# The opening of a fused attention and two-layer MLP kernel: units of 128 queries, keys turned by identity products, a new order

## The chip, the cores and the metric

One core of one Trainium2 chip runs the whole program. The metric is the device time of an execution in microseconds (us); the time before is the median of three runs.

## The reference

Attention over 4 batches, 8 heads, 768 tokens of 64 elements, in chunks of 32 queries; each chunk sees 8 memory tokens, 16 tokens to its left, its own 32 and 8 to its right. Then two dense layers on the 3072 tokens of 512 elements, 2048 wide inside; the weights come as 64-bit floats.

```python
for c in range(nc):
    scores = scale * np.matmul(q_c, k_full.transpose(0, 1, 3, 2))
    scores = scores - np.max(scores, axis=-1, keepdims=True)
    a = np.exp(scores)
    a = a / (np.sum(a, axis=-1, keepdims=True) + 1e-09)
    out[:, :, c_start:c_end] = np.matmul(a, v_full)
...
h = x @ w_in
g = np.maximum(0.01 * h, h)
x = g @ w_out
...
h = x @ w_in2
P = a[0] + a[1] * h + a[2] * h2 + a[3] * h3
Q = 1.0 + np.abs(b[0]) * np.abs(h) + np.abs(b[1]) * h2
g = P / (Q + 1e-06)
out = g @ w_out2
```

## The kernel before

Both layers run in 6 tiles of 512 tokens by 16 blocks of the hidden width. A block is one hidden product of 12 matmuls (`emit_h`, line 753: upper by upper, upper by lower and lower by upper halves of the operands, which are split into two roundings) and one output product of 12 matmuls (`emit_y`, line 811; `emit_o`, line 849, in the second layer). The order of every engine is the order in which the code is written (`manual_schedule`); nothing is planned by costs.

**The opening** is the attention of the first 512 tokens, 8 blocks of 64 queries (`FIRST`), taken two at a time as a unit `u`. For a block, `att_q` and `att_k` (lines 368, 378) turn queries (for two blocks at once) and 88 or 104 rows of keys by transposes on PE, and ACT copies them out. `att_b1` (line 460) makes the scores of 8 heads by 2 chunks in 16 small matmuls, and DVE takes the maximum and subtracts it (lines 469, 472), 256 columns at a time. For a unit, `unit_e` takes the exponential on ACT, `unit_n` normalises on DVE (lines 418 to 421), `unit_t` (line 428) turns the probabilities in four transposes, and ACT copies them in four pieces of 64 rows (line 433) into a block-diagonal tile, whose zeros POOL has set; `unit_x` (line 444) multiplies with the values over 128 rows. The result, x, is split into an upper half by ACT (line 447) and a lower half by DVE (line 448). `heat` (line 867) issues dummy products of the identity.

**The weight chain.** `pair_load` brings raw 64-bit words. A pair `n` holds two pieces, `ONE_` and `TWO_`: pair 0 the hidden blocks 0 and 1, pair 1 hidden block 2 and output block 0, pair 2 hidden 3 and output 1, pair 3 hidden 4 and output 2. Per piece: `pair_scale` (ACT, line 170), `pair_join` (DVE, three instructions, lines 177 to 180), `pair_hi` (ACT, line 188) rounds, `pair_lo` (DVE, line 194) subtracts. From pair 3 on, a pair is done in one go. Between the pieces stands `leaky`: two activations on ACT (lines 763, 764) and one subtraction on DVE (line 766) of a hidden block.

The order on PE behind the opening is: hidden blocks 0, 1, 2, output block 0, hidden 3, output 1, the turning of the next queries and keys, hidden 4. All loads are issued on the SP queue in the order written: queries and keys of all 8 blocks, the first weight piece, the values, the other weights. `copy_mem_v` on POOL puts the memory tokens' values into the value tiles ahead of their loads.

## Time and profile before

| | |
|---|---|
| median of three runs | 1149.4 us (1149.04 to 1150.69) |
| profiled execution | 1148.0 us, span 1146.2 us |
| PE busy | 1131.7 us, 99% of the span |
| DVE, ACT, POOL busy | 769.7, 631.8, 232.1 us |
| loads and stores | 131.98 MB, mean 115 GB/s |

The span runs from the first instruction to the last; the profiled execution's own time is 1.8 us longer. Times in rows count from the span's start. Busy PE means that a matmul is in flight, not that the array is full.

### The profile page before, as it was taken

What the parts mean: (1) busy time and instruction counts of PE and PEld (TensorE: products, weight loads), DVE (VectorE), ACT (ScalarE), POOL (GpSimd) and SP (SyncE); (2) the same over time, 40 slices, a digit from 0 to 9 for tenths busy, and PEclk for the clock granted to TensorE, in tenths of its full rate; (3) what the DMA queues carried; (4) which work ended last, traced back from release to release, by engine and by line L of the source; (5) the groups of instructions that cost most, each with busy time, mean ns of one, the idle gap of its engine ahead of it and who ended that gap; (6) DMA issues with size and microseconds to landing.
All of it is one profiled execution on the core that took longest, in us unless ns stands there. A gap on an engine that the chain in (4) does not pass through costs nothing.

```text
span 1146.2 us, 19651 instructions
## 1 busy us (share of the span) xinstructions
PE 1131.7 (99%) x7616; PEld 928.3 (81%) x7616; DVE 769.7 (67%) x1318; ACT 631.8 (55%) x1149; POOL 232.1 (20%) x264
## 2 busy tenths in 40 slices
PE   7999999999999999999999999999999999999998
PEld 6777788888888888888888888888888888888886
DVE  5887846555565555542345886887887888788775
ACT  4677632232232223223346876776777777777765
POOL 3000302231221322210000222222222222222222
PEclk9999999999999999999999999999999999999999
DMA  9966687797778777742342101001100100100101
GB/s 187 260 178 196 187 226 206 213 251 206 202 215 241 208 196 230 207 142 98 97 133 83 65 1 47 28 1 39 36 1 29 46 1 15 59 1 1 37 1 37
DMA packets 148472, 131.98 MB, mean 115 GB/s; under 512 B 63296, under 2 KB 118944, under 8 KB 148380
## 3 DMA queue, kind: packets, MB, share of 16 engines
q1 hardware_dynamic: 143372, 123.25, 37.6%
q0 software_dynamic: 4864, 7.45, 2.8%
q8 instruction: 60, 0.98, 0.4%
q14 instruction: 32, 0.26, 0.1%
q10 hardware_dynamic: 144, 0.03, 0.0%
HBM read 92.92 MB, written 37.75 MB: 114 GB/s over the span
## 4 chain that ended last, share of the span: by engine, by line
PE 95%; DVE 3%; ACT 1%; issue 1%; POOL 0%; DVEq 0%; POOLq 0%
PE hps L753 45%; PE acc L849 23%; PE acc L811 22%; PE psx L667 2%; PE pss L625 1%; PE pss L460 1%; PE hot L867 1%; DVE wwall L178 1%; PE psx L444 0%; PE psx L514 0%; DVE wwall L180 0%; PE psk L378 0%; DVE wwall L177 0%; ACT w L188 0%; DVE w L194 0%
## 5 line engine op out<-in xcount | busy, mean ns | idle before, releaser
L811 PE MATMUL acc<-g,w 128*128 128x512 f32 x1152 | 278.7, 391 | 0.1
L849 PE MATMUL acc<-w,g 128*128 128x512 f32 x1152 | 275.4, 389 | 0.0
L849 PEld LDWEIGHTS acc<-w,g 128*128 128x128 f32 x1152 | 216.2, 188 | 44.8
L811 PEld LDWEIGHTS acc<-g,w 128*128 128x128 f32 x1152 | 214.7, 188 | 46.1 <-ACT w L188 0.5
L763 ACT ACTIVATE g<-hps 128x512 fp32r<-128x512 f32 x96 | 57.4, 598 | 307.1 <-PE hps L753 307.1
L789 POOL TENSOR_TENSOR g<-R,g 128x512 fp32r<-128x512 f32 x96 | 124.2, 1294 | 504.4 <-ACT g L788 466.1
L753 PE MATMUL hps<-xh,w 128*128 128x512 f32 x768 | 209.0, 395 | 3.8 <-ACT pm L484 1.5
L753 PE MATMUL hps<-yh,w 128*128 128x512 f32 x768 | 204.1, 389 | 0.0
L766 DVE TENSOR_TENSOR g<-s,g 128x512 fp32r<-128x512 f32 x96 | 66.2, 690 | 177.6 <-ACT s L764 174.4
L753 PEld LDWEIGHTS hps<-xh,w 128*128 128x128 f32 x768 | 141.2, 188 | 34.6 <-ACT w L188 2.0
L753 PEld LDWEIGHTS hps<-yh,w 128*128 128x128 f32 x768 | 144.3, 188 | 29.9
L590 POOL DMA_DIRECT2D vb<-in_v_dram x128 | 83.2, 651 | 260.5 <-PE psx L667 207.9
L776 ACT ACTIVATE A<-hps 128x512 f32<-128x512 f32 x96 | 57.2, 596 | 113.9 <-PE hps L753 113.9
L792 DVE SCALAR_TENSOR_TENSOR A<-A,small,pb 128x512 f32<-128x512 f32 x96 | 72.0, 750 | 56.2 <-ACT pb L777 56.2
L753 PE MATMUL hps<-xl,w 128*128 128x512 f32 x384 | 103.0, 390 | 0.0
L753 PE MATMUL hps<-yl,w 128*128 128x512 f32 x384 | 102.6, 389 | 0.0
L783 DVE SCALAR_TENSOR_TENSOR A<-A,pb 128x512 f32<-128x512 f32 x96 | 66.5, 692 | 30.2 <-ACT pb L796 30.2
L753 PEld LDWEIGHTS hps<-xl,w 128*128 128x128 f32 x384 | 72.1, 188 | 15.7
L753 PEld LDWEIGHTS hps<-yl,w 128*128 128x128 f32 x384 | 72.1, 188 | 14.9
L778 ACT ACTIVATE R<-hps,small 128x512 f32<-128x512 f32 x96 | 75.0, 781 | 0.0
L785 DVE SCALAR_TENSOR_TENSOR R<-R,small,A 128x512 f32<-128x512 f32 x96 | 72.2, 752 | 3.4
L794 DVE SCALAR_TENSOR_TENSOR R<-R,small,hps 128x512 f32<-128x512 f32 x96 | 71.8, 748 | 3.4
(112 smaller groups left out, 1140.1 us busy)
## 6 DMA issues: line engine op xcount, KB each, us to landing
wr<-in_moe_w_in_dram SPq DMA_DIRECT2D x32, 512.0 KB
wr<-in_moe_w_out_dram SPq DMA_DIRECT2D x32, 512.0 KB
park_dram<-pb SPq DMA_DIRECT2D x16, 512.0 KB
pb<-park_dram SPq DMA_DIRECT2D x64, 128.0 KB
w_dram<-wwall SPq DMA_DIRECT2D x32, 256.0 KB
wb<-w_dram SPq DMA_DIRECT2D x32, 256.0 KB
kb<-in_k_dram SPq DMA_DIRECT2D x59, 112.0 KB
vb<-in_v_dram POOLq DMA_DIRECT2D x118, 56.0 KB, 3.3
```

What stands on the lines that cost most here:

```text
L590: nc.gpsimd.dma_start(out=vw[r + at:r + at + n, c], in_=v[bi, hs, lo:lo + n, :].rearrange("h p d -> p h d"))
L753: nc.tensor.matmul(ps[:, :n], w_[:, ws], x_[:, kk, :], start=(kk == 0 and m == 0), stop=(kk == KC - 1 and m == 2))
L763: nc.scalar.activation(out=gh, in_=ps, func=AF.Prelu, alpha=0.01)
L766: return [lambda: nc.vector.tensor_tensor(out=gl, in0=s, in1=gh.bitcast(F32), op=ALU.subtract)]
L778: nc.scalar.activation(out=R, in_=ps, func=AF.Identity, scale=ncf[:, 3:4], bias=ncf[:, 2:3])
L783: nc.vector.scalar_tensor_tensor(out=A0, in0=A0, scalar=ONE, in1=U0, op0=ALU.add, op1=ALU.mult)
L785: nc.vector.scalar_tensor_tensor(out=R0, in0=R0, scalar=ncf[:, 0:1], in1=A0, op0=ALU.add, op1=ALU.mult)
L789: nc.gpsimd.tensor_tensor(out=gl, in0=R0, in1=gh.bitcast(F32), op=ALU.subtract)
L792: nc.vector.scalar_tensor_tensor(out=A, in0=A, scalar=babs[:, 1:2], in1=U, op0=ALU.mult, op1=ALU.add)
L794: nc.vector.scalar_tensor_tensor(out=R, in0=R, scalar=ncf[:, 1:2], in1=ps, op0=ALU.add, op1=ALU.mult)
L811: nc.tensor.matmul(acc[i][d][:, :n], w_[:, ws], g_, start=(f == 0 and m == 0), stop=(f == FC - 1 and m == 2))
L849: nc.tensor.matmul(acc[i][s], g_[:, ss], w_, start=(f == 0 and m == 0), stop=(f == FC - 1 and m == 2))
```

## The change

The opening is taken in 4 units of 128 queries throughout. `unit_load` brings the keys of a unit in two loads, as packets of two tokens (512 B instead of 256 B); even and odd tokens then lie side by side in a row, and `turned` transposes them by ordinary products with a square of the identity, 16 for rows of 44 (56 and 44 in unit 0) and 16 for rows of 32. ACT copies them out in three pieces, interleaved. In `unit_s` the two chunks of a head stand side by side in a bank of 512 columns, so that maximum, subtraction, sum and product of a unit are one instruction each. The turned probabilities are copied whole by one instruction (`unit_t`), and `unit_x` multiplies each chunk by itself over 64 rows, 32 products into two banks. The zero tiles and most dummy products go. The order of the opening is new; half of the values is loaded ahead of the first weight piece. In the weight chain the subtractions of `leaky` 0, 1 and 2 and of the second piece of pair 1 go from DVE to POOL, and other steps change places.

```diff
-    room = [t[:, n] for t in early for n in range(4)]
-    rooms = {"k": kb + room[0:6], "v": vb + room[6:12], "q": room[12:16]}
+    rooms = {"k": kb, "v": vb + [early[1][:, n] for n in (2, 3)] + [early[2][:, n] for n in range(4)]}
...
+    TT = 2
+    KA, KB = (QB + LCTX) // TT + NM, QB // TT
+    KU = (CTX // TT, CTX // TT + LCTX // 4)
...
+    kroom = [two(kall), two(early[0][:, 0:2]), two(early[0][:, 2:4]), two(early[1][:, 0:2])]
+    qroom = [early[3][:, u].rearrange("p h d -> p (h d)") for u in range(4)]
+    kTs = [kT, kT2, kT34[:, 0], kT34[:, 1]]
+    half = lambda t, n: t.rearrange("p a b c d e -> p (a b c d e)")[:, n * 512:(n + 1) * 512]
+    opm = [mall.rearrange("p b c m -> p (b c m)"), mall2.rearrange("p b c m -> p (b c m)"),
+           half(pall, 0), half(pall, 1)]
+    opt = [pmore.rearrange("p n a b c d e -> p (n a b c d e)")[:, u * 512:(u + 1) * 512] for u in range(4)]
+    oqT, ops = {}, {}
...
+    def unit_load(u):
+        at = 2 * QB * u
+        pairs = lambda x, lo, n: x[0, :, lo:lo + n, :].rearrange("h (p t) d -> p h (t d)", t=TT)
+        flat = lambda t: t.rearrange("p h t d -> p h (t d)")
+        nc.sync.dma_start(out=early[3][:, u], in_=q[0, :, at:at + P, :].rearrange("h p d -> p h d"))
+        lo = max(at - LCTX, 0)
+        row, n = (lo - at + LCTX) // TT, at - LCTX + 96 - lo
+        nc.sync.dma_start(out=flat(kroom[u][row:row + n // TT]), in_=pairs(k, lo, n))
+        nc.sync.dma_start(out=flat(kroom[u][P // 2:P // 2 + KB]), in_=pairs(k, at - LCTX + CTX, QB))
+        if u == 0:
+            nc.sync.dma_start(out=kroom[u][48:48 + NM, :, 0, :], in_=mem_k[0].rearrange("h p d -> p h d"))
...
+    def turned(ps, t, r0, rows):
+        for p in range(NP):
+            for i in range(TT):
+                r = slice(r0, r0 + rows[i])
+                for e in range(2):
+                    nc.tensor.matmul(ps[e * 64:e * 64 + 64, p, i, :rows[i]], t[r, 2 * p + e, i, :], ident[r, r],
+                                     start=True, stop=True)
...
+    def unit_ka(u):
+        rows = (48 + NM, CTX // TT) if u == 0 else (CTX // TT, CTX // TT)
+        ps = psw.tile([P, 512], F32, tag="ps", name="psk")[:, :NP * TT * rows[0]]
+        ps = ps.rearrange("p (c t m) -> p c t m", c=NP, t=TT)
+        turned(ps, kroom[u], 0, rows)
+        a, b = kTs[2 * (u % 2)], kTs[2 * (u % 2) + 1]
+        O = QB // TT
+        def first():
+            if u == 0:
+                for t in (a, b):
+                    nc.scalar.copy(out=ends(t), in_=ps[:, :, 0, 48:].unsqueeze(2).to_broadcast([P, NP, 2, NM]))
+            nc.scalar.copy(out=a[:, :, NM:NM + CTX].rearrange("p c (m t) -> p c m t", t=TT),
+                           in_=ps[:, :, :, :CTX // TT].rearrange("p c t m -> p c m t"))
+            nc.scalar.copy(out=b[:, :, NM:NM + CTX - QB].rearrange("p c (m t) -> p c m t", t=TT),
+                           in_=ps[:, :, :, O:CTX // TT].rearrange("p c t m -> p c m t"))
+        return first
+    def unit_kb(u):
+        ps = psw.tile([P, 512], F32, tag="ps", name="psk")[:, :NP * QB]
+        ps = ps.rearrange("p (c t m) -> p c t m", c=NP, t=TT)
+        turned(ps, kroom[u], P // 2, (KB, KB))
+        b = kTs[2 * (u % 2) + 1]
+        return lambda: nc.scalar.copy(out=b[:, :, NM + CTX - QB:NM + CTX].rearrange("p c (m t) -> p c m t", t=TT),
+                                      in_=ps.rearrange("p c t m -> p c m t"))
...
+    def unit_s(u, b):
+        if b == 0:
+            ops[u] = psa.tile([P, 512], F32, tag="acc", name="pss").rearrange("p (b i c m) -> p b i c m", b=2, i=2, c=2)
+        ps, qt, kt = ops[u], oqT[u], kTs[2 * (u % 2) + b]
+        for p in range(NP):
+            for e in range(2):
+                r = slice(e * 64, e * 64 + 64)
+                for c in range(2):
+                    o = e * 64 + (p % 2) * CHUNK
+                    at = b * QB + c * CHUNK
+                    nc.tensor.matmul(ps[o:o + CHUNK, b, p // 2, c, :], qt[r, p, at:at + CHUNK],
+                                     kt[r, p, c * KOFF:c * KOFF + WIN], start=True, stop=True)
+    def unit_m(u):
+        ps = ops.pop(u)
+        if u == 0:
+            nc.vector.memset(ps[:, 0, :, 0, NM:NM + LCTX], NEG)
+        ps = ps.rearrange("p b i c m -> p (b i c) m")
+        mx = tmp.tile([P, 2 * NP, 1], F32, tag="mx", name="mx")
+        nc.vector.tensor_reduce(out=mx, in_=ps, op=ALU.max, axis=AX.X, negate=True)
+        nc.vector.tensor_tensor(out=opm[u].rearrange("p (n m) -> p n m", m=WIN), in0=ps,
+                                in1=mx.to_broadcast([P, 2 * NP, WIN]), op=ALU.add)
...
+    def unit_t(u):
+        ps = psa.tile([P, 512], F32, tag="acc", name="pst")
+        for i in range(4):
+            nc.tensor.transpose(ps[:, i * P:(i + 1) * P], opm[u][:, i * P:(i + 1) * P], ident)
+        return lambda: nc.scalar.copy(out=opt[u], in_=ps)
...
+    def unit_x(u, pool, tag):
+        ps = [pool.tile([P, 512], F32, tag=tag, name="psx")[:, :NP * QB].rearrange("p (n b m) -> p n b m", n=NP, b=2)
+              for c in range(2)]
+        pt = opt[u].rearrange("p (b i e h m) -> p b i e h m", b=2, i=2, e=2, h=2)
+        for b in range(2):
+            vt = rooms["v"][2 * u + b]
+            for p in range(NP):
+                for c in range(2):
+                    r = slice(c * SB, c * SB + SB)
+                    for e in range(2):
+                        nc.tensor.matmul(ps[c][e * 64:e * 64 + 64, p, b, :], vt[r, 2 * p + e, :],
+                                         pt[r, b, p // 2, e, p % 2, :], start=True, stop=True)
+        xh, xl = (x[:, :, 2 * QB * u:2 * QB * (u + 1)].rearrange("p n (b c m) -> p c n b m", b=2, c=2) for x in xt[0])
+        def upper():
             for c in range(2):
+                nc.scalar.copy(out=xh[:, c], in_=ps[c])
+        def under():
+            for c in range(2):
+                nc.vector.tensor_tensor(out=xl[:, c], in0=ps[c], in1=xh[:, c].bitcast(F32), op=ALU.subtract)
+        return upper, under
...
+    def leaky(c, eng=nc.vector):
...
-        nc.vector.memset(kb[0][0:32], 0.0)
+        nc.vector.memset(kroom[0][0:32], 0.0)
...
+        U = FIRST // 2
+        for u in range(U):
+            unit_load(u)
+        for j in range(4):
+            load_v(j)
         pair_load(0, ONE_)
+        xt[0] = (xpool.tile([P, KC, NMAX], F32R, tag="xh", name="xh"),
+                 xpool.tile([P, KC, NMAX], F32R, tag="xl", name="xl"))
+        heat(6)
+        unit_q(0)
+        key_a = unit_ka(0)
+        key_b = unit_kb(0)
+        key_a()
+        key_b()
+        for t in (2, 3):
+            nc.gpsimd.tensor_copy(out=ends(kTs[t]), in_=ends(kT))
+        copy_mem_v(early[2][:, 0:3])
+        for j in range(4, FIRST):
             load_v(j)
         pair_load(0, TWO_)
         pair_load(1)
         heat(2)
+        unit_s(0, 0)
+        unit_q(1)
+        unit_s(0, 1)
+        key_a = unit_ka(1)
+        key_a()
+        unit_m(0)
+        unit_e(0)
+        key_b = unit_kb(1)
+        unit_q(2)
+        key_b()
+        unit_n(0)
+        unit_s(1, 0)
+        key_a = unit_ka(2)
+        key_a()
+        unit_s(1, 1)
+        key_b = unit_kb(2)
+        key_b()
+        unit_m(1)
+        unit_e(1)
+        unit_s(2, 0)
+        unit_s(2, 1)
+        unit_m(2)
+        key_a = unit_ka(3)
+        key_a()
+        unit_q(3)
+        turned_p = unit_t(0)
+        key_b = unit_kb(3)
+        key_b()
+        turned_p()
+        unit_e(2)
+        unit_n(1)
+        unit_s(3, 0)
+        unit_s(3, 1)
+        turned_p = unit_t(1)
+        turned_p()
+        unit_m(3)
+        x0 = unit_x(0, psw, "ps")
+        x0[0]()
+        unit_n(2)
+        unit_e(3)
+        x1 = unit_x(1, psw, "ps")
+        turned_p = unit_t(2)
+        turned_p()
         pair_scale(0, ONE_)
+        unit_n(3)
+        x1[0]()
+        x0[1]()
+        turned_p = unit_t(3)
+        turned_p()
+        run(pair_join(0, ONE_))
+        x2 = unit_x(2, psa, "acc")
+        x2[0]()
+        pair_hi(0, ONE_)
+        pair_lo(0, ONE_)
+        x3 = unit_x(3, psa, "acc")
+        x3[0]()
+        x3[1]()
+        x1[1]()
+        x2[1]()
...
+        nc.gpsimd.memset(pall, 0.0)
...
         emit_h(0)
         pair_scale(0, TWO_)
-        pair_scale(1, ONE_)
         run(pair_join(0, TWO_))
         pair_hi(0, TWO_)
+        pair_scale(1, ONE_)
+        pair_lo(0, TWO_)
         run(pair_join(1, ONE_))
-        pair_lo(0, TWO_)
-        steps = leaky(0)
+        run(leaky(0, nc.gpsimd))
         pair_hi(1, ONE_)
         pair_scale(1, TWO_)
         pair_lo(1, ONE_)
         emit_h(1)
         run(pair_join(1, TWO_))
-        run(steps)
-        steps = leaky(1)
         pair_hi(1, TWO_)
         pair_scale(2, ONE_)
-        pair_lo(1, TWO_)
+        pair_lo(1, TWO_, nc.gpsimd)
+        run(leaky(1, nc.gpsimd))
         emit_h(2)
         run(pair_join(2, ONE_))
-        run(steps)
-        steps = leaky(2)
+        run(leaky(2, nc.gpsimd))
         pair_hi(2, ONE_)
         pair_scale(2, TWO_)
         pair_lo(2, ONE_)
         run(pair_join(2, TWO_))
-        run(steps)
         pair_hi(2, TWO_)
         pair_scale(3)
         pair_lo(2, TWO_)
```

On PE, in the middle of the opening (`kT`, `kT_105`, `kT_106` are turned keys, `pm` and `pb` probabilities, `hot` dummies). Before:

```order
L368 MATMUL psq<-ident,early 128x128 x4
L378 MATMUL psk<-ident,early 128x88 x8
L867 MATMUL hot<-ident 128x128
L428 MATMUL pst<-ident,pm_105 128x128 x4
L460 MATMUL pss<-kT,qT 32x64 x16
L460 MATMUL pss<-kT_106,qT 32x64 x16
L867 MATMUL hot<-ident 128x128 x4
L428 MATMUL pst<-ident,pm 128x128 x4
L444 MATMUL psx<-pb,vb 64x64 x16
L867 MATMUL hot<-ident 128x128 x2
```

and now:

```order
L423 MATMUL psk<-ident,early 64x44 x16
L470 MATMUL pss<-kT_106,qT 32x64 x16
L423 MATMUL psk<-ident,early 64x32 x16
L470 MATMUL pss<-kT,qT 32x64 x16
L470 MATMUL pss<-kT_105,qT 32x64 x16
L423 MATMUL psk<-ident,early 64x44 x16
L429 MATMUL psq<-ident,early 128x128 x4
L498 MATMUL pst<-ident,pm 128x128 x4
L423 MATMUL psk<-ident,early 64x32 x16
L470 MATMUL pss<-kT_106,qT 32x64 x32
L498 MATMUL pst<-ident,pm_104 128x128 x4
```

The turning of probabilities (`pst`) stood ahead of the next unit's scores (`pss`); now the scores of units 1 and 2 stand ahead of the first of them, and the keys (`psk`) take two groups of 16 between them.

On DVE, in the weight chain from the second piece of pair 1 on (`wr_93` pair 1, `wr_94` pair 2, `w` the lower half, `g` the hidden block). Before:

```order
L194 TENSOR_TENSOR w<-wwall,w 128x512 x2
L177 TENSOR_SCALAR wwall<-wwall 128x512
L178 SCALAR_TENSOR_TENSOR wwall<-wr_93,wwall 128x512
L180 SCALAR_TENSOR_TENSOR wwall<-wr_93,wwall 128x512
L766 TENSOR_TENSOR g<-s,g 128x512
L194 TENSOR_TENSOR w<-wwall,w 128x512
L177 TENSOR_SCALAR wwall<-wwall 128x512
L178 SCALAR_TENSOR_TENSOR wwall<-wr_94,wwall 128x512
L180 SCALAR_TENSOR_TENSOR wwall<-wr_94,wwall 128x512
L766 TENSOR_TENSOR g<-s,g 128x512
L194 TENSOR_TENSOR w<-wwall,w 128x512
L177 TENSOR_SCALAR wwall<-wwall 128x512
```

and now, from the lower half of pair 0's second piece on:

```order
L194 TENSOR_TENSOR w<-wwall,w 128x512
L177 TENSOR_SCALAR wwall<-wwall 128x512
L178 SCALAR_TENSOR_TENSOR wwall<-wr_93,wwall 128x512
L180 SCALAR_TENSOR_TENSOR wwall<-wr_93,wwall 128x512
L194 TENSOR_TENSOR w<-wwall,w 128x512
L177 TENSOR_SCALAR wwall<-wwall 128x512
L178 SCALAR_TENSOR_TENSOR wwall<-wr_93,wwall 128x512
L180 SCALAR_TENSOR_TENSOR wwall<-wr_93,wwall 128x512
L177 TENSOR_SCALAR wwall<-wwall 128x512
L178 SCALAR_TENSOR_TENSOR wwall<-wr_94,wwall 128x512
L180 SCALAR_TENSOR_TENSOR wwall<-wr_94,wwall 128x512
L194 TENSOR_TENSOR w<-wwall,w 128x512
```

The subtractions into `g` have left DVE, and so has one into `w`; two joins now stand in a row.

On POOL, behind the copies of the memory values, now (before, two memsets stood there and then the loads of later values):

```order
L345 COPY early<-early 32x1024
L968 COPY kT_106<-kT 128x4x2x8 x2
L345 COPY early<-early 8x1536
L345 COPY early<-early 32x1536
L1043 MEMSET pb 128x1024
L833 TENSOR_TENSOR g<-s,g 128x512
L194 TENSOR_TENSOR w<-wwall,w 128x512
L833 TENSOR_TENSOR g<-s,g 128x512 x2
L656 DMA vb<-in_mem_v_dram 8x4x64
```

The four subtractions stand behind the memset of the probabilities' tile.

## Rows read from the trace of the kernel before

**Rows 1.** Page, parts 1 and 4: busy time of each engine; the chain by engine.

```profile
PE 1131.7 (99%) x7616; PEld 928.3 (81%) x7616; DVE 769.7 (67%) x1318; ACT 631.8 (55%) x1149; POOL 232.1 (20%) x264
...
PE 95%; DVE 3%; ACT 1%; issue 1%; POOL 0%; DVEq 0%; POOLq 0%
```

**Rows 2.** Waits of PE, 54 us to the end: us in total, times, longest.

```profile
PE hps L753 <- ACT pm L484: 1.5, 2, 0.8
```

**Rows 3.** Timeline of PE, 0 to 57 us: start, us, what, count, idle before.

```profile
5.28 0.93 PE L378 MATMUL psk<-ident,kb 104*128 104x104 f32 x4
...
13.34 0.60 PE L368 MATMUL psq<-ident,early 128*128 128x128 f32 x4
13.78 0.86 PE L378 MATMUL psk<-ident,early 88*128 88x88 f32 x8
...
16.07 0.63 PE L428 MATMUL pst<-ident,pm 128*128 128x128 f32 x4 [1.17 <-DVE pm L421]
16.63 1.10 PE L460 MATMUL pss<-kT,qT 64*32 64x64 f32 x64
...
34.49 1.19 PE L753 MATMUL hps<-xh,w 128*128 128x512 f32 x4 [0.47 <-ACT xh L447]
...
54.29 1.20 PE L753 MATMUL hps<-xh,w 128*128 128x512 f32 x4 [1.33 <-ACT w L188]
```

**Rows 4.** Timeline of DVE, 0 to 62 us.

```profile
1.55 0.48 DVE L873 MEMSET kb<- 32x512 f32 x1 [0.16 <-issue]
...
12.48 0.43 DVE L469 TENSOR_REDUCE mx<-pss 128x4 f32<-128x256 f32 x1 [1.88 <-PE pss L460]
...
14.08 0.68 DVE L418 TENSOR_REDUCE sm<-pm 128x8 f32<-128x512 f32 x1
...
15.23 0.69 DVE L421 TENSOR_TENSOR pm<-pm,sm 128x512 f32<-128x512 f32 x1
17.35 0.43 DVE L469 TENSOR_REDUCE mx<-pss 128x4 f32<-128x256 f32 x1 [1.42 <-PE pss L460]
...
23.45 0.42 DVE L472 TENSOR_TENSOR pm<-pss,mx 128x256 f32<-128x256 f32 x1
...
34.47 0.42 DVE L448 TENSOR_TENSOR xl<-psx,xh 128x256 fp32r<-128x256 f32 x1 [0.35 <-ACT xh L447]
35.04 0.43 DVE L177 TENSOR_SCALAR wwall<-wwall 128x512 uint32<-128x512 uint32 x1
...
36.84 0.42 DVE L177 TENSOR_SCALAR wwall<-wwall 128x512 uint32<-128x512 uint32 x1
...
49.95 0.69 DVE L177 TENSOR_SCALAR wwall<-wwall 128x1024 uint32<-128x1024 uint32 x1 [0.35 <-ACT wwall L170]
```

**Rows 5.** Timeline of ACT, 0 to 62 us.

```profile
26.50 1.50 ACT L433 COPY pmore<-pst 64x256 f32<-64x256 f32 x4 [1.90 <-PE pst L428]
...
41.92 0.62 ACT L188 CAST w<-wwall 128x512 fp32r<-128x512 f32 x1
42.45 0.67 ACT L170 ACTIVATE wwall<-wr 128x512 f32<-128x512 f32 x1
...
53.19 1.04 ACT L188 CAST w<-wwall 128x1024 fp32r<-128x1024 f32 x1 [2.31 <-DVE wwall L180]
```

**Rows 6.** Timeline of PE: probabilities times values, three forms of the product.

```profile
26.34 1.15 PE L444 MATMUL psx<-pb,vb 128*64 128x64 f32 x32
...
173.44 1.41 PE L667 MATMUL psx<-pm,vb 64*64 64x32 f32 x64
...
195.07 1.14 PE L667 MATMUL psx<-pm,vb 64*64 64x32 f32 x64
```

**Rows 7.** Line 789 on POOL: shortest, median, longest in ns, first and last start.

```profile
L789 POOL TENSOR_TENSOR g<-R,g x96: 1283/1294/1307, 623.7 to 1138.1; 128x512 fp32r<-128x512 f32 x96
```

**Rows 8.** Windows: length, PEclk (granted clock), DMA share, GB/s.

```profile
2.00:16.00 14.00, 1.00 1.10 195
16.00:38.00 22.00, 1.00 1.06 275
```

More of the change, by code (lines that the diff above doesn't have):

```diff
@@ L379, in att_k @@
         pv = ps[:, :NP * rows].rearrange("p (c m) -> p c m", c=NP)
-        nc.scalar.copy(out=keys(j)[:, :, NM:NM + CTX], in_=pv[:, :, :CTX])
+        nc.scalar.copy(out=kT[:, :, NM:NM + CTX], in_=pv[:, :, :CTX])
         if j % BPS == 0:
-            for t in (kT, kT2) if j == 0 else (kT,):
-                ends = t.rearrange("p c (g m) -> p c g m", m=NM)[:, :, 0:KW // NM:KW // NM - 1, :]
-                nc.scalar.copy(out=ends, in_=pv[:, :, KLOAD:].unsqueeze(2).to_broadcast([P, NP, 2, NM]))
+            nc.scalar.copy(out=ends(kT), in_=pv[:, :, KLOAD:].unsqueeze(2).to_broadcast([P, NP, 2, NM]))
     def att_a(j):
```

141 lines of the change are left out of this document (26 added, 115 removed).

## The prediction

> **What bounds the kernel now.** I read the page first: the busy times and the chain of waits [rows 1]. TensorE (PE) is busy 99% of the span and 95% of the chain lies on it, so work taken off another engine is worth something only where PE waits for it. The waits of PE after 54 us [rows 2] show how little that is later: their largest group is 1.5 us, the next is the wait of 1.33 that ends at 54.29 [rows 3]. So nearly all that can be won lies ahead of 54.29, where PE starts hidden block 4 of the first layer [rows 3]. I call that start **the gate**: behind it both programs have PE's instructions in the same order, so the time changes by what the gate moves.
>
> In the timelines of PE, VectorE (DVE) and ScalarE (ACT) up to the gate, the reader sees two stretches. The opening (attention of the first 512 queries) has a period of 4.86 us per pair of blocks (DVE's first maximum at 12.48, then 17.35 [rows 4]), of which DVE works 3.4; the rest is the detour over PE, where the turning of the probabilities (16.07) stands ahead of the next scores (16.63) and waits for DVE's last product [rows 3]. The last subtraction of a row's maximum ends at 23.45 + 0.42 = 23.87, the last lower half of x at 34.47 + 0.42 = 34.89 [rows 4]. Then the weight chain: DVE joins the words of six weight pieces, ACT rounds them, DVE subtracts; it ends in ACT's rounding of pair 3 at 53.19 [rows 5], which releases the gate 1.1 us later.
>
> **Step 1, scores: 2.6 us earlier.** The first keys come later. Their tile's memset has 1024 columns instead of 512, twice 0.48 [rows 4], and the keys' load waits for it, with every later load behind it on SP; one more load stands ahead of mem_k. That is 0.5 to 0.9 us behind the 5.28 of before [rows 3]; I take 5.9. Loads after that don't bind at first: before, the load engines moved 195 GB/s [rows 8]; a unit of 128 queries now brings 0.33 MB of keys in pieces of 512 B for 0.39 MB in pieces of 256 B.
>
> From 5.9 PE itself sets the pace, because the scores no longer stand behind the turning of probabilities. Turning keys by identity products takes 16 products of about 44x64 by 44 columns, and 16 by 32 columns, per unit, where eight transposes took 0.6 (13.78, 0.86 with its drain [rows 3]). No row has this form. Below: 32 products of 64x64 by 32 columns took 1.14 and 1.41 with a drain of 0.1 (195.07, 173.44 [rows 6]), so 16 take 0.52 at best. Above: 16 of 128x64 by 64 columns took 1.15, again with its drain (26.34 [rows 6]): 1.09 as I count it. I take 0.75 and 0.62, nearer to the first, whose size is closer. The scores keep their sizes, and two groups of 16 took 1.10 [rows 3]; but neighbours in the order now write the same 32 rows of the bank where they wrote different ones. Bounds 0.52 and again 1.09; I take 0.65, nearest to the unchanged shape.
>
> Sum on PE: unit 0's keys at the slow rate of the first 7 us (four transposes at 5.28 took 0.93, eight at 13.78 took 0.86 [rows 3]) 1.3, then 0.62; two dummy products 0.55; three query turnings of 0.44 (13.34 to 13.78 [rows 3]); three times 0.75 and three times 0.62 for keys; one turning of probabilities 0.55; eight score groups of 0.65: 13.65 us, to 19.55; with 0.15 of waiting for ACT's key copies 19.7. DVE keeps up: three units of maximum and subtraction at 1.45 and two normalisations at 1.76 from 10.5 end at 18.4. Unit 3's maximum and subtraction over 512 columns take 0.7 each, as the 512-wide sum (0.68 [rows 4]): 21.2 against 23.87. Eight pieces of 256 become four of 512, which by itself saves DVE only 0.3 per unit.
>
> **Step 2, from there to x: 1.5 us.** DVE then does two normalisations (14.08 to 15.92 [rows 4], 1.76 each from start to next start, 3.5), two lower halves of x over 256 columns (0.42 each, of which I let 0.09 lie under the next one), the join of the first weight piece (1.85), waits 0.8 for ACT's rounding, subtracts (0.6), and six lower halves (2.0): 9.5 to 30.7, against 11.0 before. What goes is the stall behind four copies of 64 rows each, 1.50 for one pair [rows 5]; one whole copy of 512 columns replaces them. Next late here is unit 3's product with the values: PE turns its probabilities at 24.9, works 2 x 1.25 for units 2 and 3 (between 1.04 and 1.31, the two rows of the same form [rows 6]), ACT copies until 28.7, the moment at which DVE gets there. The values of unit 3 are the last load: 1.05 MB of queries, 1.29 of keys, 0.52 of weights and 1.79 of values at 195 GB/s end at 25.9, under one us ahead of their product.
>
> **Step 3, the weight chain: 1.3 us longer.** Four subtractions go to GpSimd (POOL), four times 0.6 off DVE. But now DVE has nothing to put between a join and the subtraction that waits for ACT. Five joins of 1.84 (35.04 to 36.84 [rows 4], and a handover) 9.2; pair 3's join, twice as wide, 3.2 (49.95 [rows 4] to 53.19 [rows 5]); four subtractions 2.4; four waits for ACT's 0.62 rounding with its handovers [rows 5], 0.68 each, 2.7; one wait for rounding and scaling in a row (0.62 and 0.67 [rows 5]), 1.3; one for pair 3's scaling 0.5. Together 19.3, and 0.1 to 0.2 of starts; before, 35.04 to 53.19 was 18.15. Behind each of DVE's waits stand the next joins, and behind those PE's hidden blocks. PE isn't late in between: its product for output block 0 waits for POOL's first weight subtraction until about 41, the gate has 1.1 us of slack over that path.
>
> A subtraction on POOL takes 1.29 [rows 7]. What it costs DVE, no row of the opening shows: nothing as the lower bound, 1.29 each as the upper (DVE standing still meanwhile). I take 0.2 in all: the 96 later ones took 1283 to 1307 ns whatever ran beside them [rows 7].
>
> The dummy products that go, the memsets that go from POOL (its copies of memory values, ahead of the last values' loads on SP, end near 11 us, before SP is there) and the first-value loads ahead of the first weights lie beside other work: PE is fuller than before without the dummies, and the granted clock reads 1.00 from 2 to 38 us [rows 8], also past PE's gap of 1.17 us ahead of 16.07 [rows 3].
>
> **Sum.** 2.6 + 1.5 - 1.3 - 0.2 = 2.6 us. The profiled execution took 1148.0 with a span of 1146.2; the median of three is 1149.4. From the median: 1146.8. A difference under 0.2%, 2.3 us, can't be told from none here, so the forecast lies just past that edge.
>
> **Rivals.**
> (a) *Nothing that can be told.* Scores at 0.75 instead of 0.65 cost 0.8, keys in the middle of their bounds 0.9: about 1148.5; values 0.5 late at unit 3 add as much. For it: three prices that no row has, none with slack behind it. Against: the sizes are nearest to the cheap rows. 0.38.
> (b) *Slower, PE becomes the bound.* At the upper price, 1.09, eight score groups cost 8 x 0.44 and the seven warm groups of key products about 7 x 0.4 more, 6.3 in all: 1153.1. It decides from 41% of that price on, where the gain is gone. Against: scores and key products have half the rows and no more columns than the dear row. 0.07.
> On this the Trainium skill ("TensorE: Matmul & The Clock Gate", The mechanism) has a rule: a weight load overlaps with matmuls in flight only when the row group differs. All sixteen key products of a group lie in one row group. By that rule case (b) would be the likelier for the keys; the dear row, with all 128 rows, bears it out, no row of 64 does.
> (c) *Slower, POOL holds DVE up.* If DVE stands still for the four subtractions, 4 x 1.29 = 5.2 is lost, 0.2 of it counted above: 1151.8; from about half of that on the gain is gone. For it: the joins beside them read two operands from SBUF, and one of the four gates PE's output block 0. Against: the narrow spread in rows 7. 0.07.
> The Trainium skill ("GPSIMD Engine Reference", Specifications) states just that: GpSimd's SBUF interfaces are shared with VectorE, with contention against instructions that have two SBUF inputs. It gives no price, and no trace here has that pair side by side.
>
> **How the numbers follow.** The forecast has 0.48, (a) 0.38, (b) and (c) 0.14 together. The forecast's own range: scores and keys at their lower bounds give 2.0 more and POOL free 0.2, so 1144.6, to 1147.1, where the edge lies. The range goes from 1144.2, a little below, for an earlier first key, through all of (a) to 1150.4, half of (b) or (c). Faster 0.48, same 0.38, slower 0.14.
>
> **What would show it.** Right: the gate near 51.7; the last subtraction of a maximum ending near 21.2, the last lower half of x near 30.7, and 19 to 20 us from there to the rounding of pair 3, with DVE waiting for ACT four times 0.7. PE without a gap between the first keys and unit 3's scores. Wrong: score groups or key products near 1.1; a gap ahead of unit 3's value product (loads); DVE's joins longer than 1.84 while POOL works; or any new wait of PE behind the gate.

## The result and the profile after

The changed kernel took 1163.58 us (median of 4, 1160.22 to 1167.66) against 1149.4: ratio 1.0123, interval 1.0082 to 1.0163. It is slower by 14 us; 1146.8 was forecast. The profiled execution took 1160.95 with a span of 1158.6, 12.4 more than before, and the gate (PE L820 here) moved from 54.29 [rows 3] to 65.88, 11.6 later. So the loss lies ahead of the gate, where the prediction had put the gain.

The page of the changed kernel, its part 1 (to be held against [rows 1]), and the windows of PE in it (length, busy with count, granted clock, DMA share, GB/s; against [rows 8]):

```profile
PE 1144.0 (99%) x7920; PEld 937.2 (81%) x7920; DVE 770.2 (66%) x1308; ACT 628.4 (54%) x1144; POOL 235.6 (20%) x267
```

```profile
2.00:16.00 14.00, 12.68 (x259) 0.88 1.05 188
16.00:38.00 22.00, 20.84 (x512) 0.57 0.89 245
38.00:46.00 8.00, 7.27 (x77) 0.50 1.16 277
```

PE has 304 records more (7920 for 7616), all in the opening. The granted clock, 1.00 in these stretches before, is at its lower level (0.50, which is 1.2 GHz) from 10 to 12 us and from 20 to 46 us. The timeline of PE in the changed kernel answers to [rows 3]:

```profile
6.47 2.18 PE L423 MATMUL psk<-ident,kb 56*64 56x56 f32 x64 [1.32 <-DMA kb<-in_mem_k_dram]
...
15.18 0.69 PE L470 MATMUL pss<-kT,qT 64*32 64x64 f32 x32
15.79 1.13 PE L423 MATMUL psk<-ident,early 44*64 44x44 f32 x32
16.85 0.69 PE L470 MATMUL pss<-kT,qT 64*32 64x64 f32 x32
17.47 1.11 PE L423 MATMUL psk<-ident,early 32*64 32x32 f32 x31
19.25 0.21 PE L423 MATMUL psk<-ident,early 32*64 32x32 f32 x1 [0.67 <-issue]
19.39 1.95 PE L470 MATMUL pss<-kT,qT 64*32 64x64 f32 x64
21.27 1.94 PE L423 MATMUL psk<-ident,early 44*64 44x44 f32 x32
...
26.89 1.95 PE L470 MATMUL pss<-kT,qT 64*32 64x64 f32 x64
...
65.88 1.21 PE L820 MATMUL hps<-xh,w 128*128 128x512 f32 x4 [1.36 <-ACT w L188]
```

Sixteen key products (32 records: each product makes two) take 1.06 us at the full clock (15.79 to 16.85) and 1.87 at the lower (21.27 to 23.14). Unit 3's scores end at 28.77. DVE in the changed kernel, its last maximum, its last lower halves of x and the joins beside POOL (against [rows 4]):

```profile
1.66 0.91 DVE L944 MEMSET kb<- 32x1024 f32 x1 [0.26 <-issue]
...
29.66 0.69 DVE L480 TENSOR_TENSOR pb<-pss,mx 128x512 f32<-128x512 f32 x1
...
40.08 2.08 DVE L521 TENSOR_TENSOR xl<-psx,xh 128x256 fp32r<-128x256 f32 x6 [0.23 <-ACT xh L517]
42.08 0.42 DVE L177 TENSOR_SCALAR wwall<-wwall 128x512 uint32<-128x512 uint32 x1
42.53 0.69 DVE L178 SCALAR_TENSOR_TENSOR wwall<-wr,wwall 128x512 uint32<-128x512 uint32 x1
43.26 0.69 DVE L180 SCALAR_TENSOR_TENSOR wwall<-wr,wwall 128x512 uint32<-128x512 uint32 x1
...
52.10 1.03 DVE L177 TENSOR_SCALAR wwall<-wwall 128x512 uint32<-128x512 uint32 x1 [1.26 <-ACT wwall L170]
53.17 1.79 DVE L178 SCALAR_TENSOR_TENSOR wwall<-wr,wwall 128x512 uint32<-128x512 uint32 x1
55.00 1.65 DVE L180 SCALAR_TENSOR_TENSOR wwall<-wr,wwall 128x512 uint32<-128x512 uint32 x1
```

and POOL and ACT beside them (the second against [rows 5]):

```profile
51.57 1.28 POOL L194 TENSOR_TENSOR w<-wwall,w 128x512 fp32r<-128x512 f32 x1 [3.07 <-ACT w L188]
53.12 2.98 POOL L833 TENSOR_TENSOR g<-s,g 128x512 fp32r<-128x512 f32 x2 [0.27 <-ACT s L831]
```

```profile
64.78 1.04 ACT L188 CAST w<-wwall 128x1024 fp32r<-128x1024 f32 x1 [2.31 <-DVE wwall L180]
```

The three instructions of a join sum to 1.80 us at 42.08 and to 4.47 at 52.10, while POOL subtracts. From the first join behind x to pair 3's rounding it is 22.7 us (42.08 to 64.78) where it was 18.15.

### The profile page after: what moved, and what is told of

It is laid out like the page before. It is cut to its first block, busy times and chain, and to the rows that moved or that the text cites. A ratio compares the mean times of both kernels' runs of the same rounds, so it can differ in the third digit from the quotient of the medians.

```text
span 1158.6 us, 20243 instructions
## 1 busy us (share of the span) xinstructions
PE 1144.0 (99%) x7920; PEld 937.2 (81%) x7920; DVE 770.2 (66%) x1308; ACT 628.4 (54%) x1144; POOL 235.6 (20%) x267
## 4 chain that ended last, share of the span: by engine, by line
PE 95%; DVE 2%; ACT 1%; DMA 1%; issue 1%; SPq 0%; DVEq 0%
PE hps L820 45%; PE acc L916 23%; PE acc L878 22%; PE psx L734 2%; PE pss L692 1%; PE psk L423 1%; PE pss L470 1%; DVE wwall L178 0%; PE psx L511 0%; PE pss L534 0%; PE psx L581 0%; DVE wwall L180 0%; DMA pb<-park_dram 0%; DVE wwall L177 0%; DMA park_dram<-pb 0%
## 5 line engine op out<-in xcount | busy, mean ns | idle before, releaser
L820 PE MATMUL hps<-xh,w 128*128 128x512 f32 x768 | 211.4, 399 | 5.8 <-ACT w L188 3.2
L820 PE MATMUL hps<-yh,w 128*128 128x512 f32 x768 | 204.1, 389 | 0.0
L820 PEld LDWEIGHTS hps<-xh,w 128*128 128x128 f32 x768 | 142.7, 190 | 37.7 <-ACT w L188 3.8
L820 PEld LDWEIGHTS hps<-yh,w 128*128 128x128 f32 x768 | 144.2, 188 | 30.0
L820 PE MATMUL hps<-xl,w 128*128 128x512 f32 x384 | 104.1, 393 | 0.0
L820 PE MATMUL hps<-yl,w 128*128 128x512 f32 x384 | 102.6, 389 | 0.0
L820 PEld LDWEIGHTS hps<-xl,w 128*128 128x128 f32 x384 | 72.5, 189 | 16.3 <-DVE xl L521 0.5
L820 PEld LDWEIGHTS hps<-yl,w 128*128 128x128 f32 x384 | 72.1, 188 | 14.9
```

The costliest lines, as they stand in the source:

```text
L820: nc.tensor.matmul(ps[:, :n], w_[:, ws], x_[:, kk, :], start=(kk == 0 and m == 0), stop=(kk == KC - 1 and m == 2))
```

## The experiments

Medians, and ratios to the kernel before on the same chip. The runs were made in five batches (e1 to e4, e5 to e8, e9 to e12, e13 to e15, e16 and e17), each on a chip of its own; the median of the kernel before was 1148.70 to 1149.14 in all of them, so a difference of medians between batches is good to about half a us, beside the runs' own spread. Traces show one execution of each.

| run | us | ratio, interval |
|---|---|---|
| e1 weight chain of before | 1157.04 | 1.0077 (1.0049 to 1.0104) |
| e2 dummies in the change | 1166.06 | 1.0149 (1.0119 to 1.0179) |
| e3 keys of before | 1150.54 | 1.0014 (1.0005 to 1.0024) |
| e4 before without dummies | 1148.42 | 0.9999 (0.9989 to 1.0008) |
| e5 keys and chain of before | 1146.58 | 0.9980 (0.9971 to 0.9990) |
| e6 e3, subtractions on DVE | 1149.59 | 1.0003 (0.9993 to 1.0012) |
| e7 key products by turns | 1192.91 | 1.0381 (1.0365 to 1.0397) |
| e8 e7, chain of before | 1189.3 | 1.0347 (1.0332 to 1.0362) |
| e9 equal rows, by turns | 1155.98 | 1.0065 (1.0049 to 1.0080) |
| e10 equal rows, in turn | 1157.8 | 1.0083 (1.0065 to 1.0102) |
| e11 e5, POOL subtracts | 1150.03 | 1.0011 (1.0000 to 1.0021) |
| e12 e5, three dummies | 1148.0 | 0.9994 (0.9984 to 1.0004) |
| e13 e5, many small dummies | 1156.84 | 1.0067 (1.0043 to 1.0092) |
| e14 e5, few large dummies | 1152.86 | 1.0028 (1.0015 to 1.0041) |
| e15 e5 again | 1146.74 | 0.9977 (0.9968 to 0.9987) |
| e16 e5, four wide dummies | 1147.87 | 0.9996 (0.9985 to 1.0007) |
| e17 e13, places apart | 1155.47 | 1.0053 (1.0033 to 1.0073) |

**Halves undone: e1, e3, e5.** e1 is the change with the weight chain's order and its subtractions as before:

```diff
-        run(leaky(0, nc.gpsimd))
+        steps = leaky(0)
...
-        pair_lo(1, TWO_, nc.gpsimd)
+        pair_lo(1, TWO_)
```

> The changed kernel with the weight chain written as before (the four subtractions back on DVE, steps in the old places). Theory POOL: the subtractions on POOL slow DVE's joins beside them (1.03, 1.79, 1.65 us where 0.42, 0.69, 0.69 stood) and leave waits; with them back the joins return to 0.42, 0.69, 0.69, the chain from the last lower half of x to the rounding of pair 3 goes from 22.7 to 18 to 18.5 us, and the time is 4 us less than the change, about 1159. Theory clock alone: the chain lengthens only as far as PE is late, the time stays within 1 us of the change's for like clocks.

e3 loads and turns the keys as before, one token a packet, and leaves the rest of the change:

```diff
-        turned(ps, kroom[u], 0, rows)
...
+            nc.tensor.transpose(ps[:, p * rows:(p + 1) * rows], s[:rows, p * P:(p + 1) * P], ident[:rows, :rows])
```

> The changed kernel with keys loaded in packets of one token and turned by transposes as before; the rest is the change's. Theory PE price: groups of keys take 0.3 us of PE instead of 1.06 at full clock, scores of unit 3 come 5 to 6 us earlier, time 1153 to 1157. Theory clock: with even less work on PE and no dummies the clock still falls to 0.50 somewhere between 10 and 45 us, and half of the gain or more is lost: 1156 to 1162.

e5 has both edits.

> The change with both suspects undone: keys turned four at a time by transposes as before, and the weight chain in the order of before with its subtractions on DVE. Theory (two separate costs that add up): e3 had its last xl end at 33.6 us, 1.3 us ahead of the kernel before, and lost 22.5 - 18.9 = 3.6 us in the chain behind it; with the chain of before the gate comes 3.6 us ahead of e3, near 53.9, and the time near 1147 us (1146 to 1148.5), 2 us below the kernel before. Rival (the costs are not separate: the narrow score and value products hold TensorE at the lower granted clock and this alone sets the gate): time stays within 1 us of e3, 1149.5 to 1151.5.

Against the change, the chain of before gives 6.5 us, the keys of before 13.0, both 17.0. In e1 the joins read 0.42, 0.69 and 0.69 again and the chain takes 18.9 (41.59 to 60.46), as the theory of POOL had it; the time fell by 2 us more than its 4, within the spread of e1's runs (1151.85 to 1162.16). e3 came out below both of its forecasts. e5 came as its first theory had it. What then is left of the change (units of 128 queries, score chunks side by side, whole copies of probabilities, the rest of its order and loads) beats the kernel before by 2.6 us (e5), and by 2.2 again (e15): the only version whose interval lies below 1. e5's DVE and ACT rows show where the forecast's terms came true:

```profile
21.02 0.69 DVE L474 TENSOR_TENSOR pb<-pss,mx 128x512 f32<-128x512 f32 x1
...
32.32 0.43 DVE L177 TENSOR_SCALAR wwall<-wwall 128x512 uint32<-128x512 uint32 x1
```

```profile
50.79 1.04 ACT L188 CAST w<-wwall 128x1024 fp32r<-128x1024 f32 x1 [2.30 <-DVE wwall L180]
```

The last maximum is subtracted by 21.71 (21.2 was forecast, 23.87 before [rows 4]), and the chain takes 18.5 (18.15 before). The last lower half of x ends near 32.3, not 30.7.

**The weight chain: e6, e11.** e6 is e3 with the four subtractions back on DVE, in the new order.

```diff
-        run(leaky(0, nc.gpsimd))
+        run(leaky(0))
```

> e3 with the new order of the weight chain left in, but its four subtractions given back to DVE. Theory (DVE slows beside POOL's subtractions: 1.04, 1.79 and 1.65 us for a join that takes 0.42, 0.69 and 0.69 elsewhere, 2.7 us; and 1.02 for 0.69 once): all joins of 512 columns read 0.42, 0.69, 0.69, the gate comes about 3 us ahead of e3's 57.5, and the time is about 3 us below e3 and 0.6 us above e5, near 1147.5. Rival (the new order alone costs it, POOL is only where the wait shows): the time stays within 1 us of e3, 1149.5 to 1151.5, and e5 alone is faster.

The time came where the rival had it, not the theory: e6 is 1.0 us below e3 and 3.0 above e5. The joins do read 0.42, 0.69, 0.69 again, as the theory had it. So the run does not split order from POOL cleanly, since DVE now does the hidden tiles' subtractions where POOL did them, and one stands ahead of a join and waits for ACT:

```profile
43.27 0.70 DVE L827 TENSOR_TENSOR g<-s,g 128x512 fp32r<-128x512 f32 x1 [0.85 <-ACT s L825]
```

Wait and subtraction are 1.5 of e6's chain of 21.05 us (32.84 to 53.89); without them 19.5 would be left, the prediction's figure for this order; no run shows the order with these subtractions off both engines.

e11 asks the other way: e5 in the order of before, with these subtractions on POOL.

```diff
-        steps = leaky(1)
+        steps = leaky(1, nc.gpsimd)
```

> e5 (keys and weight chain of before) with nothing changed but that three subtractions of the hidden tiles and one of the weights run on POOL. Theory (what DVE loses beside POOL is more than the four subtractions that it saves): some DVE joins of 512 columns read 1.0, 1.7 and 1.7 us in place of 0.42, 0.69 and 0.69, a POOL subtraction takes 1.3 us or more, the gate comes 1 to 4 us later than e5's 51.9, time 1147.5 to 1150.5. Rival (in e3 the joins were only slow because that order left them beside two POOL subtractions at once; otherwise POOL's work lies beside idle DVE): gate within 0.6 us of e5's, time 1146 to 1147.3.

3.4 us slower than e5, as the first theory had it. DVE in e11:

```profile
40.84 1.03 DVE L177 TENSOR_SCALAR wwall<-wwall 128x512 uint32<-128x512 uint32 x1 [1.25 <-ACT wwall L170]
41.91 1.67 DVE L178 SCALAR_TENSOR_TENSOR wwall<-wr,wwall 128x512 uint32<-128x512 uint32 x1
43.62 1.66 DVE L180 SCALAR_TENSOR_TENSOR wwall<-wr,wwall 128x512 uint32<-128x512 uint32 x1
```

POOL's pair of subtractions ran from 41.55 for 3.17 beside them. The join loses 2.6 us. The four subtractions saved on DVE give back little: DVE waits for ACT instead (1.25 ahead of 40.84, then 0.68 and 0.69).

**Dummies and the clock: e2, e4, e12.** e2 puts 28 dummy products (128x128) between the groups of the changed opening, e4 takes all but the first six out of the kernel before.

```diff
         unit_s(0, 1)
+        heat(2)
```

> The changed kernel with 30 dummy products put back between the groups of the opening. Theory clock: the granted clock stays at 1.00 from 10 us to the first hidden block, the opening ends 6 to 10 us earlier although PE gets 8 us more work, the time is 1153 to 1158 and the spread between runs shrinks. Theory PE price (narrow products are simply dear, the clock follows something else): the clock still falls to 0.50, and the time rises by up to 8 us, to 1168 to 1172.

> The kernel before with all dummies of the opening taken out but the first six. Theory clock: the granted clock falls to 0.50 in the opening of this kernel too, and the time rises by 4 to 12 us. Rival (the dummies don't matter, the narrow key products bring the clock down): clock 1.00, time within 1 us of before, 1148 to 1150.

Neither forecast for e2 came: dummies gain nothing in the change (+2.5 us within intervals that overlap), though the clock read 1.00 from 9 to 19 and from 25 to 34 us. Unit 3's maximum began at 29.32, no earlier than at 28.93 in the change. PE in e2:

```profile
9.91 0.69 PE L470 MATMUL pss<-kT,qT 64*32 64x64 f32 x32
...
22.82 1.22 PE L934 MATMUL hot<-ident 128*128 128x128 f32 x4
...
27.96 1.29 PE L470 MATMUL pss<-kT,qT 64*32 64x64 f32 x64
29.18 0.71 PE L934 MATMUL hot<-ident 128*128 128x128 f32 x4
```

From the first scores to the end of unit 3's, start to start, it is 19.3 us (9.91 to 29.18), of which the dummies in between take 3.6. The other groups, the same as in the change, take 15.7 where the change took 19.2 (9.53 to 28.77). So the clock is worth some 3.6 us of PE there, and the dummies that bring it back take as much: e2 does not clear the clock as a cause. It is not the whole cause either: the four runs of the change had mean clocks of 0.987, 0.997, 0.987 and 0.985 for 1161, 1168, 1160 and 1166 us, so the run with the best clock was the slowest.

In e4 the time was the rival's, but not its clock of 1.00: it fell to 0.50 from 16 to 18 and from 26 to 28 us, and the kernel before lost nothing by it.

e12 fills the wait of e5 (1.71 us) behind which its clock falls.

```diff
         turned_p = unit_t(2)
         turned_p()
+        heat(3)
```

> e5 with three dummy products put into the 1.7 us in which TensorE waits ahead of the last turning of probabilities. Theory (that wait is what lets the granted clock fall to 0.50 just behind it, so the last 128 value products took 3.14 us in place of 2.2): the clock reads 1.00 there, the last value products take 2.2 us, the gate comes 0.5 to 1 us earlier, time 1145.5 to 1146.5. Rival (the small products let the clock fall whatever stands between them, or DVE's subtractions bound that stretch anyway): the gate stays within 0.4 us of 51.9 and the time within 0.7 us of 1146.6.

The clock read 1.00 from 24 to 31 us, where e5 has 0.55 from 27 to 31; but PE waited 0.89, 0.18 and 1.67 us without a releaser (0.65 in e5), and the time rose by 1.4. The first theory was right about the clock and wrong about the time.

**The key products: e7 to e10.** e7 makes the products of both key groups by turns, one on partitions 0 to 43, one on 64 to 95; e8 adds the chain of before.

```diff
+                    for ps, r0, rows in parts:
+                        r = slice(r0, r0 + rows[i])
+                        nc.tensor.matmul(ps[e * 64:e * 64 + 64, p, i, :rows[i]], t[r, 2 * p + e, i, :],
+                                         ident[r, r], start=True, stop=True)
```

> The change with the two groups of key products of a unit made as one, a product on partitions 0 to 43 and one on partitions 64 to 95 by turns, and nothing else. Theory (a product whose stationary operand lies on the same rows as the one before waits for it: 66 ns each; the scores, which change rows, take 38 ns): 32 products take 1.1 to 1.25 us at the full clock where they took 2.2, the last scores come 3 to 4 us earlier for four units (twice that where the clock is at half), and the time falls by 4 to 8 us to 1155 to 1160. Rival (each small product has its own fixed price wherever its rows lie): 2.1 to 2.2 us per 32 at the full clock, time within 2 us of 1163.6.

> e7 with the weight chain of before as well (order and subtractions on DVE). Theory: both gains add, so e7 less about 5 us: 1150 to 1155; if it comes below 1149 the key packets are worth keeping. Rival (fixed price per product): as e1, 1155 to 1159.

Both theories fell. PE in e7:

```profile
22.38 11.48 PE L424 MATMUL psk<-ident,early 44*64 44x44 f32 x64
```

359 ns a product. The operands change between 44 and 32 rows at every step. The Trainium skill ("TensorEngine Tiling (Array Packing)", Key Properties) says that changing the tiling mode, and not only the tile, drains the engine; e9 bears that out, which loads both blocks' packets alike, 44 rows from partition 0 and 44 from 64, with the chain of before (the edit below is e9's, against the change). e10 is e9 with one block's products ahead of the other's.

```diff
-        nc.sync.dma_start(out=flat(kroom[u][P // 2:P // 2 + KB]), in_=pairs(k, at - LCTX + CTX, QB))
+        nc.sync.dma_start(out=flat(kroom[u][P // 2:P // 2 + CTX // TT]), in_=pairs(k, at - LCTX + QB, CTX))
...
+        turned(kroom[u], (ps, 0, rows), (pb, P // 2, half_rows))
```

> e1 (the change with the weight chain of before) with the packets of a unit's two query blocks laid out alike, 44 rows from partition 0 and 44 from partition 64 (12 packets are loaded twice), and their products made by turns. e7's products by turns took 360 ns each; they changed between 64 and 32 rows at every step. Theory (changing the number of rows the array is split into empties it, 0.3 us a time; with equal splits, products that change rows overlap as the scores do): 33 to 40 ns a product at the full clock, 1.1 to 1.3 us for the 32 of a unit, as eight transposes cost 0.9; the time falls from e1's 1157 to 1147 to 1151. Rival (alternating rows is dear whatever the sizes): 32 products near 11 us as in e7, time near 1189. Second rival (a fixed price per product): 2.1 us per 32, time 1154 to 1158.

> e9's layout with the products of the first query block ahead of those of the second, so that only one product of 32 changes rows. Theory (a product waits for the one before it where both lie on the same rows): 66 ns a product at the full clock, 2.1 us per 32, time 1153 to 1158, some 5 us above e9. Rival (order makes no difference): the same time as e9 within 1.5 us.

PE in e9:

```profile
12.45 1.15 PE L424 MATMUL psk<-ident,early 44*64 44x44 f32 x64
...
15.52 0.69 PE L462 MATMUL pss<-kT,qT 64*32 64x64 f32 x31 [1.07 <-issue]
...
20.16 1.17 PE L462 MATMUL pss<-kT,qT 64*32 64x64 f32 x65 [2.28 <-issue]
...
24.37 0.26 PE L424 MATMUL psk<-ident,early 44*64 44x44 f32 x2 [1.97 <-issue]
...
35.51 2.57 PE L503 MATMUL psx<-pmore,early 64*64 64x32 f32 x90 [0.93 <-issue]
```

Products on changing rows take 33 ns (1.07 us for 32), on the same rows 56 (e10: 15.13 to 16.93 for 32). The Trainium skill ("TensorE: Matmul & The Clock Gate", The mechanism) has a weight load overlap with products in flight only where the row group differs; the two prices agree with it. But at half the price the time hardly fell (1.1 us from e1, intervals overlapping), short of the 1147 to 1151 of e9's theory: in place of the products PE waits 6.25 us with no releaser that the profile shows (1.68 in e1), and its first keys came 1.06 later (7.48 for 6.42). e10 has its dearer products again and only 2.35 of such waits, and is 1.8 us slower than e9, not 5.

**TensorE's instructions: e13 to e17.** Those waits have a pattern. Counting the records of PE's timeline from the start, they stood here:

```
after  347                     e9   221 347 474 726     e13  474 600 725
e1     474 726                 e10  347 474 726         e14  471 596
e2     222 347 727             e11  219                 e16  596
e3     219 470                 e12  344 470 596         e17  600 725
e5     219 345
```

Steps of 126 records, whatever is computed there (e4, e6, e7, e8 and e15 have none; the kernel before has one, of 0.48 us at 438, that fits no such step). And in every run of the list a packet of 16 KB in the instruction queue ends 1.3 to 1.8 us before each such wait does. The load queues of e9 from 22.00 to 22.25 us (packets, MB, share of 16 engines), ahead of the wait that ended at 24.37:

```profile
q8 instruction: 1, 0.02, 23.3%
q1 hardware_dynamic: 11, 0.01, 20.6%
```

So PE waits for its own code. The Trainium skill ("Runtime: NRT & Kernel Launch", Instruction fetch mechanics) has blocks of 16 KiB, 256 instructions. A record is a weight load and a product, so by that figure a block is an estimated 128 records, near the 126 seen. The same place of the Trainium skill calls the crossing mostly hidden; here it cost up to 3.5 us. To tell code from busy time, e13 adds 28 small dummies behind each unit's keys in e5, e14 three of 128x128, e16 one of 128x512, and e17 gives e13's dummies columns of their own. The edits of e13, then of e16:

```diff
         key_b = unit_kb(0)
+        small(28)
```

```diff
         key_b = unit_kb(0)
+        nc.tensor.matmul(hot, ident, qroom[0], start=True, stop=True)
```

> e5 with 28 dummy products of 44 rows by 44 columns behind each unit's keys, on rows 0 and 64 by turns: 56 records more a unit, which at e9's 17 ns a record is 0.95 us of TensorE, and no other work or load. Theory (TensorE's instructions arrive in blocks: its gaps without a releaser stood at records 220, 346, 472 and 726 in every kernel that had them, a packet of 16 KB in the instruction queue ahead of each, and e9 had no less than 4.2 us from one such gap's end to the next): the 224 records are 1.8 blocks more, gaps without a releaser sum to 3 us or more at those counts, and the time rises by 4 to 8 us over e5, to 1151 to 1155. Rival (only TensorE's busy time counts): up to 3.8 us if all of it is on the path, the same as with the few large ones of the next run, 1147 to 1150.

> e5 with three dummy products of 128 rows by 128 columns in the same four places: 6 records more a unit, 0.85 to 0.95 us of TensorE. Theory (blocks of instructions): the same TensorE time without the code, so no new gaps without a releaser, and 0 to 3 us over e5, 1146.5 to 1149.5, at least 3 us below the run with many small products. Rival (busy time counts): as the run with many small ones, within 1.5 us.

> e5 unchanged, beside the two runs that add dummies to it, and once more against the kernel before: 1145.5 to 1148, ratio to before 0.997 to 0.999. If its interval takes in 1.000, the gain of the version with the keys and the weight chain of before is not shown.

> e14 with one dummy product of 512 columns in place of three of 128 in each of the four places: about the same TensorE time (0.87 to 1.0 us a unit), 2 records a unit in place of 6, 600 to the first hidden product in place of 616. Theory (what e14 lost is waits for instructions: 3.28 us at record 471 and 3.52 at 596, and record 472 falls behind the turning of probabilities with 16 records fewer): the first of the two waits goes, the time falls below e14's 1152.9 by 2 us or more, to 1147 to 1151. Rival (busy time of TensorE): the same as e14 within 1 us.

> e13 with each small dummy product writing columns of its own. In e13 they took 33 ns a record, 1.83 us for a unit's 56, twice what was meant, as if each waited for the one before it on the same place; so e13 and e14 did not have the same TensorE time and did not tell code from busy time. Theory (code): at 17 ns a record (0.95 us a unit, as e14) it still loses more than e14, 1154 to 1158, with waits without a releaser of 4 us or more in sum. Rival (busy time): as e14, 1151 to 1154. If the products still take 33 ns a record the run tells nothing of this.

e13 adds as many records as the key products do, and loses 10.1 us against e15, more than its theory's 4 to 8: all that the key products lose (e1 less e5, 10.5), with the keys, their loads and their copies as before. But its dummies took 33 ns a record (1.83 us a unit, in e17 too, which so tells nothing of its question), so e13 against e14 doesn't separate code from busy time. Most of what e13 and e17 lose is busy time. The first products with values, in e13, e17 and e15:

```profile
28.71 0.90 PE L505 MATMUL psx<-pmore,vb 64*64 64x32 f32 x48
```

```profile
26.19 0.90 PE L505 MATMUL psx<-pmore,vb 64*64 64x32 f32 x48
```

```profile
20.33 1.14 PE L505 MATMUL psx<-pmore,vb 64*64 64x32 f32 x64
```

They begin 8.4 us (e13) and 5.9 us (e17) later than in e15, with one wait for code of 0.65 and none ahead of them.

e14, with the large dummies, fits neither forecast: it has two waits for code where none was expected, and costs 6.1 us against e15. e14 against e16 shows what such waits alone cost. PE in e14, then in e16:

```profile
25.93 0.44 PE L505 MATMUL psx<-pmore,early 64*64 64x32 f32 x9 [3.28 <-issue]
...
34.92 0.85 PE L505 MATMUL psx<-pmore,early 64*64 64x32 f32 x20 [3.52 <-issue]
```

```profile
20.02 1.06 PE L999 MATMUL hot<-early,ident 128*128 128x512 f32 x2
...
32.64 0.42 PE L505 MATMUL psx<-pmore,early 64*64 64x32 f32 x4 [0.73 <-issue]
```

e16 keeps PE busy longer for a unit (0.99 us, 20.02 to 21.01; e14's three take 0.80) but has 16 records fewer ahead of the first hidden product, and is 5.0 us faster by the medians (3.7 by the ratios), as its theory had it. e14's first products with values began at 20.71, 0.4 after e15's; its loss is the two waits, 6.8 us. So for e14 busy time falls as the cause, and waits for code can cost the kernel what they last. Ahead of its second, long wait the load queues of e14 show, from 26 to 32.5 us:

```profile
DMA packets 2533, 1.83 MB, mean 281 GB/s; under 512 B 1379, under 2 KB 2431, under 8 KB 2533
...
q1 hardware_dynamic: 2533, 1.83, 95.6%
```

PE passed record 472 at 25.9, just as the weights' loads of 512 KB began; no instruction packet moved before 32.5. In e15 it passed the same count at 25.8, and a packet moved at 28.35, although four loads of weights had been issued in between there too. That e14's packet stood behind the weights in the queues is possible, but no run shows it; why it came so much later stays open.

## Why the prediction was wrong

**Step 1 failed**, with two of its terms: the price of the key products, and the full clock that it counted on without the dummies. Forecast: the last maximum subtracted at 21.2; it ended at 30.35. Against the sum's own terms PE lost 9.2 us in the profiled execution, start to start: key products of units 1 to 3 took 8.8 for 4.1, of which 2.3 is price (1.06 and about 1.09 for 0.75 and 0.62), 0.7 the wait for code and 1.7 the clock; scores 6.9 for 5.2, query turnings 2.5 for 1.3, the turned probabilities and dummies 0.8 more, most of it at the lower clock; 0.6 a later first key (6.47 for 5.9), 0.2 unit 0's keys. By kind that is about 5.4 us of groups slower than at the full clock, 2.3 of price, 0.7 of waiting for code and 0.8 of a later start. This is an account of one execution; runs bear out its parts (e2 the clock, with 3.6 us of these groups; e9 the price; e3 and e5 that without the key products the loss goes), but none splits them in the change itself.

The price was the case of rival (b) for the keys; the score groups held theirs (0.61 at the full clock for 0.65). But (b) at its full 6.3 us would have given 1153.1. What no case had is the clock, and that PE's instructions are themselves a supply. In the change's own trace the supply is only 0.7 us; it is what kept cheaper key products from paying, since e9 halves their price and waits 6.25 us for code. Two of the prediction's own signs of being wrong came: key products near 1.1, and DVE's joins longer than 1.84 beside POOL.

**The dummies and the clock.** "The granted clock reads 1.00 from 2 to 38 us, also past PE's gap of 1.17" was read as if the clock would hold without them. In the change it read 0.50 from 10 to 12 us, after a gap of 1.32 (ahead of 6.47), and from 20 us on, after one of 0.67 (ahead of 19.25), shorter than the gap that had been taken as harmless. A gap by itself does not settle it: behind 0.99 (ahead of 11.90) the clock fell to 0.51 in e12 (14 to 16 us), behind 0.95 (ahead of 11.26) it stayed at 1.00 in e15. That dummies cost nothing to leave out was still right for the time of the kernel before (e4), and to put them back does not help (e2).

**Step 2** forecast 9.5 us from there to x, ending at 30.7. In the change it took 11.8 (30.35 to 42.16), 2.3 more, with PE at the lower clock all along (0.50 from 30 to 42 us); in e5, without the key products, it took 10.6, with PE's last 128 value records partly at the lower clock (3.14 us; 2.11 in e11, where it read 1.00). Steps 1 and 2 were to give 4.1 us; e5 gives 2.6.

**Step 3, its POOL term failed.** The chain was to take 19.3 and 0.1 to 0.2 of starts; it took 22.7. By DVE's rows the order was priced rightly: those beside POOL lose 2.67 in one join (4.47 for 1.80) and 0.57 in one subtraction (47.80 took 1.26 for 0.69), and 22.7 less these 3.24 is 19.46. So POOL costs 3.2 where 0.2 was taken and rival (c) had up to 5.2. That DVE is held up beside POOL is what e11 shows by itself: 3.4 us. It agrees with the Trainium skill ("GPSIMD Engine Reference", Specifications), where GpSimd's SBUF interfaces are shared with VectorE. The later subtractions [rows 7], 1283 to 1307 ns, were a poor witness: they show what POOL's instruction takes, not what DVE's beside it does.

What held: the gate carries the time (it moved by 11.6 us, the span by 12.4); behind it 0.8 us are left.

One sum of the prediction is off, and nothing hangs on it: half of (b) is 1149.95 and half of (c) 1149.3, not the 1150.4 that bounds its range.

## What to carry to other kernels

An engine's instructions are a load like any other: where many small products stand close together, count records as well as nanoseconds, and look for waits without a releaser that stand at equal counts. Handing an instruction to an idle engine is not free to the one beside it: price it by what the neighbour's instructions take meanwhile. A granted clock read in a kernel full of dummies does not carry over to one without them. And undo a change by parts: two parts of this one cost 17 us and hid that the rest gains 2 to 3.
